# Fused mLSTM, soft-MoE and MLP kernel: the first two chunks' gates, k, q and v loaded apart, decay differences as a bias of the exponentials, gate transpositions in pieces

## The chip, the cores and the metric

One core of one Trainium2 chip. The metric is the device time of one execution in microseconds (us), as a median over runs.

## What is computed

Three stages in a row, in fp32. The first is an mLSTM recurrence over 768 steps for 4 batches of 8 heads with 40 columns each:

```python
m_new = np.maximum(f_gate[:, :, t] + m, i_gate[:, :, t])
f_stab = np.exp(f_gate[:, :, t] + m - m_new)
i_stab = np.exp(i_gate[:, :, t] - m_new)
C = f_stab[..., None, None] * C + i_stab[..., None, None] * np.einsum('bhd,bhe->bhde', vt, kt)
n = f_stab[..., None] * n + i_stab[..., None] * kt
y[:, :, t] = o * np.einsum('bhde,bhe->bhd', C, qt) / np.maximum(np.abs(nq), 1.0)
```

where `nq` is n times q, and `o` the sigmoid of `o_gate`. The 3072 rows of 320 that come out go through a soft mixture of 8 experts with 4 slots each (inner width 1024), and then through an MLP of width 2048 with a squared relu: `g = max(x @ w_in, 0)**2; out = g @ w_out`.

## The kernel before, in words

The recurrence is not stepped. The 768 steps are cut into 6 chunks of 128. The 32 pairs of batch and head go in 11 groups of up to 3 heads. A unit is one group and one chunk. Inside a unit the kernel works with 128 x 128 decay matrices; from chunk to chunk it carries the state. The groups 0 and 1 come first, and their 12 units go by pairs of chunks: chunks 0 and 1 of group 0, of group 1, then chunks 2 and 3 of both, then chunks 4 and 5. Group by group follow the others, then the experts and the MLP.

Before any unit can start, the gates must become decays. `prep(c0, c1)` holds these steps for a stretch of chunks: "1" is chunks 0 and 1, "2" is 2 and 3, "3" is 4 and 5. All operands have 96 rows, three copies of the 32 heads. The letters are:

- f: running sum of the forget gate in each chunk (VectorE scan, L359); i: input gate minus that sum (VectorE, L375); m: running maximum (a copy of the border columns and a scan on VectorE, L364 and L365);
- h, r, u, l, v: the negated maximum in three bf16 parts, stacked in `M3` (L387 on ScalarE, L381 on VectorE, L394 on ScalarE, L375 on VectorE, L396 on ScalarE);
- p: maximum carried in from the chunk before (L370); b and a: differences with the last maximum of the chunk and with the carried one (both are the `sub` helper, L375; b on VectorE, a on GpSimd, as its "G" says); B and A: their exponentials (ScalarE, L378, one instruction for all columns);
- q: TensorE turns the three blocks of 32 rows of each chunk into columns with one 96-wide transposition per chunk (L355), and ScalarE copies both to `qt3` (L356). Column block 0 of `qt3` is the bias of the unit's exponentials, block 1 weighs v, block 2 scales the carried part.

`prep_dec` ("D") makes the carried decay of two chunks in four pieces (L403 and L404, L407, L415 on TensorE, L423).

The units' steps have letters too: M copies a head's row of `M3` over 128 partitions (TensorE, L448); E takes the exponential of it with a bias (ScalarE, L462, three of 128 x 128); K masks the upper triangle (GpSimd, L469); T is k times q (TensorE, L479); P multiplies both (VectorE, L491); W weighs v (GpSimd, L435); U is k times weighted v (TensorE, L510); C is the state's update (VectorE, L526 or L541). `M4` is step M of unit 4, which is group 0 in chunk 2. "~36" is 36 short matmuls on the identity (L203), which compute nothing and only keep TensorE at work.

The order of the start is a string, `START`, written out by hand. Each engine runs its own instructions strictly in the string's order. The part ahead of the first "|" stands before the main loop; each later part is run in one turn of the loop, i = 0, 1, 2 and so on. Turn i issues M of unit i + 3, T of unit i + 2 and U of unit i + 1, then its part of `START`, then P of i + 2 and E of i + 3.

All loads are issued by SyncE (SP), in program order: both gate arrays whole (96 x 768 each, 295 KB), then for groups 0 and 1 three blocks of k, q and the token-wise v and k. The k blocks lie on the diagonal of a block matrix (`kbd`), which must be zeroed first: the first half of group 0 by VectorE (L285), three other quarters by ScalarE (L288, each 120 x 1152). k and q come in two halves of 384 columns.

Of the kernel before, what the change touches and what calls it, by code (L numbers as in the profile page):

```python
# [44 lines left out]
def kernel(  # L45
# [240 lines left out]
    for g, cs in ((1, halves[0]), (0, halves[1]), (1, halves[1])):  # L286
        z = kbd[g][:, :, cs]
        nc.scalar.activation(z, ident[0 : 3 * D, 0:1].unsqueeze(2).to_broadcast(list(z.shape)), AF.Copy, scale=0.0)  # L288
    for g in range(2):
        load_kb(g, halves[0])  # L290
        load_q(g, halves[0])
        load_kv(g)
    for g in range(2):
        load_kb(g, halves[1])
        load_q(g, halves[1])
    nc.sync.dma_start(out=phs, in_=phi)
    load_x(0, range(NC))
# [42 lines left out]
    def prep(c0, c1):  # L340
# [8 lines left out]
        last = mm[32:64, cs, L - 1 : L].to_broadcast([32, w, L])  # L349
# [2 lines left out]
        def qt():
            t = ltb
            for c in range(c0, c1):
                nc.tensor.transpose(t[:, 96 * (c - c0) : 96 * (c - c0) + 96], q3[:, c, :], ident[0:96, 0:96])  # L355
            nc.scalar.copy(qt3[:, cs, :], t[:, 0 : 96 * w].rearrange("p (c s) -> p c s", s=96))  # L356
# [1322 lines left out]
```

## Time and profile before

| | |
|---|---|
| median of 3 runs | 376.58 us (375.27 to 377.73) |
| profiled execution | 376.6 us |
| its span in the trace | 374.9 us |
| TensorE busy | 364.6 us, 97% |
| VectorE, ScalarE, GpSimd busy | 263.5, 258.5, 102.8 us |
| granted TensorE clock | full speed in all 40 slices of the page |

The span runs from the first to the last instruction that the trace shows; 1.7 us of the execution lie around it. A timeline row gives the start in us, the duration in us, the engine, the line, the operation, its output and input with their shapes, and how many instructions were merged; brackets give the idle time ahead of it and what ended that.

### The profile page before, as it was taken

What the parts mean: (1) busy time and instruction counts of PE and PEld (TensorE: products, weight loads), DVE (VectorE), ACT (ScalarE), POOL (GpSimd) and SP (SyncE); (2) the same over time, 40 slices, a digit from 0 to 9 for tenths busy, and PEclk for the clock granted to TensorE, in tenths of its full rate; (3) what the DMA queues carried; (4) which work ended last, traced back from release to release, by engine and by line L of the source; (5) the groups of instructions that cost most, each with busy time, mean ns of one, the idle gap of its engine ahead of it and who ended that gap; (6) DMA issues with size and microseconds to landing.
All of it is one profiled execution on the core that took longest, in us unless ns stands there. A gap on an engine that the chain in (4) does not pass through costs nothing.

```text
span 374.9 us, 10814 instructions
## 1 busy us (share of the span) xinstructions
PE 364.6 (97%) x4203; PEld 325.1 (87%) x4203; DVE 263.5 (70%) x597; ACT 258.5 (69%) x594; POOL 102.8 (27%) x205
## 2 busy tenths in 40 slices
PE   8999999998899999999999999999999999999996
PEld 6789888888779885345999999999999999999995
DVE  8879889986998587886799655555555555555551
ACT  7798776678566865766798756676675666667661
POOL 5576986775687573000000000000000000000000
PEclk9999999999999999999999999999999999999999
DMA  5887998999979999893000200020020001002002
GB/s 183 266 315 217 344 328 238 298 332 347 295 199 397 311 353 365 313 380 130 2 0 2 70 3 0 2 71 2 0 72 1 0 11 60 3 0 73 0 2 70
DMA packets 23004, 56.73 MB, mean 151 GB/s; under 512 B 2865, under 2 KB 9865, under 8 KB 22569
## 3 DMA queue, kind: packets, MB, share of 16 engines
q1 hardware_dynamic: 22953, 56.04, 44.3%
q8 instruction: 33, 0.54, 0.6%
q14 instruction: 18, 0.15, 0.1%
HBM read 52.10 MB, written 3.93 MB: 149 GB/s over the span
## 4 chain that ended last, share of the span: by engine, by line
PE 85%; DVE 5%; ACT 4%; POOL 3%; issue 2%; POOLq 0%
PE ps_mb L1574 19%; PE ps_st L1574 17%; PE ps_lt L1574 9%; PE ps_st L479 8%; PE ps_o L1501 4%; PE ps_o L567 4%; PE ps_o L582 4%; PE ps_st L1389 2%; PE ps_m L1501 2%; ACT w L462 2%; POOL w L469 2%; PE ps_mb L448 2%; PE ps_lt L203 2%; PE ps_st L510 2%; PE ps_lt L733 2%
## 5 line engine op out<-in xcount | busy, mean ns | idle before, releaser
L1525 DVE CAST hi<-ring 128x512 fp32r<-128x512 f32 x93 | 39.7, 427 | 62.0 <-ACT ring L1524 51.8
L1526 DVE TENSOR_TENSOR los<-ring,hi 128x512 fp32r<-128x512 f32 x96 | 66.6, 693 | 9.8
L462 ACT ACTIVATE w<-ps_mb,qt 128x128 f32<-128x128 f32 x192 | 56.4, 368 | 11.5 <-PE ps_mb L448 7.0
L1506 ACT ACTIVATE ring<-ps_o 128x512 f32<-128x512 f32 x64 | 38.2, 597 | 35.0 <-PE ps_o L1501 35.0
L1524 ACT ACTIVATE ring<-ring 128x512 f32<-128x512 f32 x93 | 58.8, 632 | 3.0
L479 PE MATMUL ps_st<-par 120*128 120x128 f32 (+1 forms) x384 | 57.0, 284 | 0.7 <-DVE cu L541 0.6
L1574 PE MATMUL ps_mb<-wohlh,hi 128*128 128x320 f32 x160 | 49.4, 310 | 0.0
L1574 PE MATMUL ps_mb<-wohll,hi 128*128 128x320 f32 x160 | 49.3, 309 | 0.0
L1574 PE MATMUL ps_mb<-wohlh,los 128*128 128x320 f32 x160 | 49.2, 309 | 0.0
L479 PEld LDWEIGHTS ps_st<-par 120*128 120x128 f32 (+1 forms) x384 | 47.9, 191 | 1.2 <-PE ps_mb L448 0.9
L491 DVE TENSOR_TENSOR p<-ps_st,w 128x384 f32<-128x384 f32 (+1 forms) x66 | 35.6, 539 | 16.8 <-POOL w L469 8.2
L469 POOL TENSOR_SCALAR_AFFINE_SELECT w<-w 128x384 f32<-128x384 f32 (+1 forms) x66 | 38.3, 581 | 25.1 <-ACT w L462 23.6
L1574 PE MATMUL ps_st<-wohll,hi 128*128 128x320 f32 x144 | 44.6, 310 | 0.0
L1574 PE MATMUL ps_st<-wohlh,hi 128*128 128x320 f32 x144 | 44.5, 309 | 0.0
L1574 PE MATMUL ps_st<-wohlh,los 128*128 128x320 f32 x144 | 44.5, 309 | 0.0
L1506 ACT ACTIVATE ring<-ps_m 128x512 f32<-128x512 f32 x32 | 19.1, 598 | 19.1 <-PE ps_m L1501 19.1
L1574 PEld LDWEIGHTS ps_mb<-wohll,hi 128*128 128x128 f32 x160 | 29.9, 187 | 1.5
L1574 PEld LDWEIGHTS ps_mb<-wohlh,hi 128*128 128x128 f32 x160 | 30.0, 188 | 0.0
L1574 PEld LDWEIGHTS ps_mb<-wohlh,los 128*128 128x128 f32 x160 | 30.0, 188 | 0.0
L1574 PEld LDWEIGHTS ps_st<-wohll,hi 128*128 128x128 f32 x144 | 27.0, 187 | 2.1 <-issue 0.6
L1574 PEld LDWEIGHTS ps_st<-wohlh,los 128*128 128x128 f32 x144 | 27.1, 188 | 0.0
L1574 PEld LDWEIGHTS ps_st<-wohlh,hi 128*128 128x128 f32 x144 | 27.1, 188 | 0.0
(318 smaller groups left out, 762.2 us busy)
## 6 DMA issues: line engine op xcount, KB each, us to landing
ring<-in_w_dram SPq DMA_DIRECT2D x32, 320.0 KB
stage<-in_w_in_dram SPq DMA_DIRECT2D x10, 512.0 KB
par<-in_w_dram SPq DMA_DIRECT2D x6, 640.0 KB
ring<-in_w_dram SPq DMA_DIRECT2D x6, 640.0 KB
out_dram<-ring SPq DMA_DIRECT2D x24, 160.0 KB
par<-in_k_s_dram SPq DMA_DIRECT2D x9, 360.0 KB
x<-in_o_gate_dram SPq DMA_DIRECT2D x9, 320.0 KB
par<-in_k_t_dram SPq DMA_DIRECT2D x23, 120.0 KB
```

The costliest lines, as they stand in the source:

```text
L462: nc.scalar.activation(w[:, j, :], mb[:, 128 * j : 128 * j + 128], AF.Exp, bias=qt3[:, c, h0 + j : h0 + j + 1])
L469: nc.gpsimd.affine_select(out=w, in_=w, pattern=[[0, nh], [1, 128]], compare_op=ALU.is_ge, fill=0.0, base=0, channel_multiplier=-1)
L479: nc.tensor.matmul(st[:, 128 * j : 128 * j + 128], lhsT=kbd[g % 2][0:nd, j, ts_], rhs=qin[g][0:nd, ts_], start=True, stop=True,)
L491: nc.vector.tensor_tensor(out=p, in0=sts.pop((g, c))[:, 0 : nh * 128].rearrange("p (n t) -> p n t", n=nh), in1=ws.pop((g, c)), op=ALU.mult,)
L567: nc.tensor.matmul(pos[g, c // 2][:, o0 : o0 + nv], lhsT=qin[g][0:nd, 128 * c : 128 * c + 128], rhs=cbds[g, c - 1][0:nd], start=True, stop ...
L582: nc.tensor.matmul(po[t0 : t0 + 32, o0 : o0 + DV], lhsT=p[:, j, t0 : t0 + 32], rhs=vin[g][:, c, j, :], start=True, stop=True,)
L1501: nc.tensor.matmul(t, lhsT=gst[n][:, 128 * k : 128 * k + 128], rhs=cst[tg], start=True, stop=True)
L1506: nc.scalar.activation(r, t, AF.Relu)
L1524: nc.scalar.activation(r, r, AF.Square)
L1525: nc.vector.tensor_copy(hi, r)
L1526: eng.tensor_tensor(out=lo, in0=r, in1=hi.bitcast(F32), op=ALU.subtract)
L1574: nc.tensor.matmul(acc[u][:, 0:DM], lhsT=l_[:, 128 * u : 128 * u + 128], rhs=wohl[r_, f // 8][:, f % 8, :], start=(f == 0 and a == 0), sto ...
```

## The change

- Gates, k, q, v and token-wise k of groups 0 and 1 are loaded for chunks 0 and 1 first (256 columns); the gates of the other four chunks follow behind group 0's first k and q, and the rest of k, q and v (512 columns) behind that (`load_second`).
- The zeroing is cut along the same border and by block: ScalarE writes three blocks of 120 x 256 and three of 120 x 512; GpSimd the last three of 120 x 512. The constant tiles of GpSimd are split the same way, and four copies of the identity (`selF`) move from VectorE to GpSimd.
- Steps a and b go. The exponentials A and B take the difference as bias and scale, one chunk per instruction. A new small step n (VectorE) makes the negated last maximum.
- Besides q there are s, t and w: transpositions of row block 0 alone, of block 1 (rows 0 to 63 with the copy of 32 to 63), and of all 96 rows with the copy of block 2. s is copied by ScalarE, t and w by VectorE.
- `START` is written anew, with 32 filling matmuls in place of 55. Two small VectorE pieces (`heads`) move into it.

```diff
-START = "~36 1f 1i 1m 1h 1p 1b 1aG 1B 1r 1u 1A 1v D0 2f 1l T0 T1 1q M0 2i E0 W0 K0 D0 M1 E1 ~6 2m D0 2p 2b 2aG K1 W2 P0 2h D0 2B 2r 2u U0 P1 M2 2v E2 2A 2l K2 C0 ~7 | 3f 3i D1 ~6 | D1 2q 3m 3h 3p | D1 3b 3aG 3B 3r | 3u D1 3A 3l 3v | D2 3q | D2 | D2 | D2 X |"
+START = "~13 1f 1i 1s ~9 1m 1h 1p 1n 1r 1u 1v H D0 1l T0 M0 T1 1B 2f M1 E0 H 2i 1t K0 W0 D0 E1 ~9 2m 1A 2h P0 2r D0 2u K1 W2 U0 D0 P1 2l 2v 2p 2n M2 E2 K2 C0 L ~1 | 1w 2s 2B 3f | 2t D1 3i D1 | D1 3m 2A | D1 3h 3p 3n 2w 3r 3u | 3l 3v 3A D2 | 3s 3B 3t D2 | D2 3w | D2 X |"
...
-    nc.sync.dma_start(out=fg.rearrange("p c s -> p (c s)"), in_=f_gate)
-    nc.sync.dma_start(out=ig.rearrange("p c s -> p (c s)"), in_=i_gate)
-    halves = slice(0, S // 2), slice(S // 2, S)
+    def load_gates(c0, c1):
+        for t, src in ((fg, f_gate), (ig, i_gate)):
+            nc.sync.dma_start(
+                out=t[:, c0:c1].rearrange("p c s -> p (c s)"), in_=src[:, L * c0 : L * c1]
+            )
...
+    load_gates(0, 2)
+    halves = slice(0, 2 * L), slice(2 * L, S)
...
+    for g in (1, 0):
+        for j in range(3):
+            zero(g, j, halves[1 - g])
+    zeros = []
+    for j in range(3):
+        zeros.append(lambda j=j: nc.gpsimd.memset(kbd[1][:, j, halves[1]], 0.0))
+    load_kb(0, halves[0])
+    load_q(0, halves[0])
+    load_gates(2, NC)
+    load_kv(0, 0, 2)
+    load_kb(1, halves[0])
+    load_q(1, halves[0])
+    load_kv(1, 0, 2)
...
+        if r < 3:
+            nc.vector.tensor_copy(sel96[rs, :], ident[rs, rs])
+        nc.gpsimd.tensor_copy(selF[rs, :], ident[rs, rs])
...
+        def qt(r=0, n=96):
+            t = bank("o") if n == 64 and c0 == 0 else ltb
             for c in range(c0, c1):
...
+                nc.tensor.transpose(t[:, n * (c - c0) : n * (c - c0) + n], q3[0:n, c, :], ident[0:n, 0:n])
+            tv = t[:, 0 : n * w].rearrange("p (c s) -> p c s", s=n)
+            (nc.vector.tensor_copy if r else nc.scalar.copy)(qt3[:, cs, r:n], tv[:, :, r:])
...
-            return lambda: nc.scalar.activation(q3[r : r + 32, cs], q3[r : r + 32, cs], AF.Exp)
+            def go():
+                for c in range(c0, c1):
+                    src, b, k = (q3, mlast, 1.0) if r == 32 else (mm, mprev, -1.0)
+                    nc.scalar.activation(
+                        q3[r : r + 32, c], src[r : r + 32, c], AF.Exp, bias=b[r : r + 32, c], scale=k
+                    )
...
-            "a": sub(q3[64:96, cs], mprev[64:96, cs].to_broadcast([32, w, L]), mm[64:96, cs]),
-            "b": sub(q3[32:64, cs], q3[32:64, cs], last),
+            "n": last,
...
+            "s": qt32,
+            "t": lambda: qt(32, 64),
+            "w": lambda: qt(64),
```

On ScalarE, between the zeroing (`par`) and the first units' exponentials (`w`), there stands before (`M_112` is `M3`, `ring` holds the gates, `qt_113` is `qt3`):

```order
L387 ACTIVATE M_112<-ring 96x256
L378 ACTIVATE ring<-ring 32x256
L394 CAST M_112<-ring 32x256
L378 ACTIVATE ring<-ring 32x256
L396 CAST M_112<-ring 32x256
L404 ACTIVATE ring<-ring 32x2
L356 COPY qt_113<-ps_lt 128x192
L462 ACTIVATE w<-ps_mb,qt_113 128x128 x6
```

and with the change:

```order
L291 ACTIVATE par_71<-ident 120x256 x3
L291 ACTIVATE par_70<-ident 120x512 x3
L392 COPY qt_113<-ps_m 128x2x32
L435 ACTIVATE M_112<-ring 96x256
L441 CAST M_112<-ring 32x256
L443 CAST M_112<-ring 32x256
L454 ACTIVATE ring<-ring 32x2
L422 ACTIVATE ring<-ring 32x128 x2
L512 ACTIVATE w<-ps_mb,qt_113 128x128 x6
L422 ACTIVATE ring<-ring 32x128 x2
```

The copy of the transposed block moved ahead of h, the two decay exponentials moved behind u and v; one of them (A, the last row) stands behind the six exponentials of units 0 and 1.

On VectorE, from the step r of chunks 0 and 1 to the step l of chunks 2 and 3, whose output `M4` reads, there stands before:

```order
L403 TENSOR_TENSOR ring<-ring 32x2
L359 SCALAR_TENSOR_TENSOR ring<-ring 96x256
L375 TENSOR_TENSOR M_112<-ring,M_112 32x256
L375 TENSOR_TENSOR ring<-ring 96x256
L407 TENSOR_TENSOR ring<-ring 32x22
L364 COPY ring<-ring 96x2
L365 SCALAR_TENSOR_TENSOR ring<-ring 96x256
L370 TENSOR_TENSOR ring<-ring 96x2
L375 TENSOR_TENSOR ring<-ring 32x256
L491 TENSOR_TENSOR p<-ps_st,w 128x384
```

and with the change:

```order
L411 TENSOR_TENSOR M_112<-ring,M_112 32x256
L395 SCALAR_TENSOR_TENSOR ring<-ring 96x256
L360 COPY ring<-ring 32x120
L411 TENSOR_TENSOR ring<-ring 96x256
L386 COPY qt_113<-ps_o 128x2x32
L457 TENSOR_TENSOR ring<-ring 32x22
L400 COPY ring<-ring 96x2
L401 SCALAR_TENSOR_TENSOR ring<-ring 96x256
L541 TENSOR_TENSOR p<-ps_st,w 128x384
L429 SCALAR_TENSOR_TENSOR ring<-ring,M_112 96x256
```

The step l of chunks 0 and 1 moved ahead of the next stretch's scan, two steps (p, b) ahead of the first product P went, and two copies came in. Behind the product both orders go on with r, the copy of the carried decay, the second product and step l.

On GpSimd, at the end of its constants and up to the first mask K, there stands before:

```order
L322 MEMSET selJ 32x128
L323 COPY selJ<-ident 32x4x8
L375 TENSOR_TENSOR ring<-ring 32x256
L435 TENSOR_TENSOR wv<-par_70,qt_113 128x246
L469 AFFINE_SELECT w<-w 128x384
```

and with the change (of its zeroing only the last row):

```order
L301 MEMSET par_71 120x512 x3
L338 MEMSET hm 120x3
L339 AFFINE_SELECT hm<-hm 120x3
L342 AFFINE_SELECT hm<-hm 120x3
L345 MEMSET rmask 128x4
L347 MEMSET rmask 32x1 x4
L348 MEMSET selJ 32x128
L349 COPY selJ<-ident 32x4x8
L354 COPY selF<-ident 32x32 x4
L519 AFFINE_SELECT w<-w 128x384
```

Step a went, the zeroing and the four copies came in, and the first K stands ahead of the first W.

## Rows read from the trace of the kernel before

**Rows 1.** The page, its first line.
```profile
span 374.9 us, 10814 instructions
```
**Rows 2.** Windows: busy us of each engine, granted clock, DMA share, GB/s.
```profile
14.38:22.60 8.22, 7.72 (x152) 6.84 (x151) 7.79 (x23) 6.02 (x21) 5.29 (x9) 1.00 0.86 306
22.60:35.00 12.40, 12.40 (x281) 11.57 (x281) 9.85 (x26) 12.25 (x36) 8.71 (x17) 1.00 0.79 247
90.50:95.00 4.50, 3.15 (x64) 2.84 (x53) 1.77 (x6) 2.90 (x9) 2.59 (x7) 1.00 0.99 358
```
**Rows 3.** The chain of waits up to 30 us: start, us, what.
```profile
7.94 1.34 PE ps_st L479 x12
9.28 0.18 PE ps_lt L355 x2
...
10.79 0.71 POOL w L469
...
13.51 0.82 DVE M L375
```
**Rows 4.** Timeline, 0 to 20 us: the gates' path and units 0 to 6.
```profile
1.42 6.51 PE L203 MATMUL ps_lt<-ident 128*128 128x256 bf16 x36 [1.42 <-POOL dm L280]
...
2.20 3.25 ACT L288 ACTIVATE par<-ident 120x1152 f32<-120x1152 f32 x3
...
4.04 0.69 DVE L359 TENSOR_TENSOR_SCAN ring<-ring 96x256 f32<-96x256 f32 x1
...
4.97 0.42 DVE L375 TENSOR_TENSOR ring<-ring 96x256 f32<-96x256 f32 x1 [0.25 <-DMA ring<-in_i_gate_dram]
...
5.01 0.46 POOL L323 COPY selJ<-ident 32x32 f32<-32x32 f32 x1
...
5.56 0.69 DVE L365 TENSOR_TENSOR_SCAN ring<-ring 96x256 f32<-96x256 f32 x1
...
6.29 0.42 ACT L387 ACTIVATE M<-ring 96x256 bf16<-96x256 f32 x1 [0.84 <-DVE ring L365]
...
6.99 0.73 DVE L381 SCALAR_TENSOR_TENSOR ring<-ring,M 96x256 f32<-96x256 f32 x1
...
8.41 0.42 DVE L375 TENSOR_TENSOR M<-ring,M 32x256 bf16<-32x256 f32 x1
...
9.21 0.17 DVE L407 TENSOR_TENSOR ring<-ring 32x22 f32<-32x22 f32 x1
...
9.28 0.50 PE L448 MATMUL ps_mb<-M,sel 96*128 96x128 bf16 x6
...
9.83 1.66 ACT L462 ACTIVATE w<-ps_mb,qt 128x128 f32<-128x128 f32 x6
...
11.53 0.56 DVE L491 TENSOR_TENSOR p<-ps_st,w 128x384 f32<-128x384 f32 x1 [0.44 <-POOL w L469]
...
14.39 0.34 PE L448 MATMUL ps_mb<-M,sel 96*128 96x128 bf16 x3
...
18.84 0.33 PE L448 MATMUL ps_mb<-M,sel 96*128 96x128 bf16 x3 [0.31 <-ACT w L462]
```
**Rows 5.** Windows of TensorE in the first us, with DMA share and GB/s.
```profile
1.40:2.00 0.60, 0.58 (x3) 1.00 0.44 61
2.00:3.00 1.00, 1.00 (x7) 1.00 0.79 277
...
4.00:5.00 1.00, 1.00 (x6) 1.00 0.14 42
```
**Rows 6.** Waits of the DMA queue (SP), 0 to 60 us: total, times, longest.
```profile
SPq L213 <- ACT par L288: 1.9, 1, 1.9
```
**Rows 7.** Groups by shape: count, busy us, mean ns of one, idle before.
```profile
L305 POOL MEMSET ring<- 96x768 f32 x1 | 0.7, 727 | 0.0
...
L1506 ACT ACTIVATE ring<-ps_o 128x512 f32<-128x512 f32 x64 | 38.2, 597 | 35.0 <-PE ps_o L1501 35.0
```
**Rows 8.** Timeline at 92 us: a matmul in the middle of a group.
```profile
91.98 0.22 PE L582 MATMUL ps_o<-par,p 128*32 128x41 f32 x1 [1.35 <-issue]
```

More of the change, by code (lines that the diff above doesn't have):

```diff
@@ L281, with zero, load_second @@
     nc.scalar.activation(dm, dm, AF.Exp)
-    nc.sync.dma_start(out=fg.rearrange("p c s -> p (c s)"), in_=f_gate)
-    nc.sync.dma_start(out=ig.rearrange("p c s -> p (c s)"), in_=i_gate)
-    halves = slice(0, S // 2), slice(S // 2, S)
-    nc.vector.memset(kbd[0][:, :, halves[0]], 0.0)
[L286 to L297, printed above, removed]
+    def load_gates(c0, c1):
[3 more added lines that the diff above has]
+            )
+    def zero(g, j, cs):
+        z = kbd[g][:, j, cs]
+        nc.scalar.activation(z, ident[0 : 3 * D, 0:1].to_broadcast(list(z.shape)), AF.Copy, scale=0.0)
+    load_gates(0, 2)
+    halves = slice(0, 2 * L), slice(2 * L, S)
+    nc.vector.memset(kbd[0][:, :, halves[0]], 0.0)
+    for g in (1, 0):
[11 more added lines that the diff above has]
+    load_kv(1, 0, 2)
+    def load_second():
+        for g in range(2):
+            load_kb(g, halves[1])
+            load_q(g, halves[1])
+            load_kv(g, 2, NC)
+        nc.sync.dma_start(out=phs, in_=phi)
+        load_x(0, range(NC))
     nc.gpsimd.memset(gj, 1.0)
@@ L304 @@
     rst = gt(96, [NC, L])
-    nc.gpsimd.memset(rst, 1.0)
-    nc.gpsimd.memset(rst[:, :, 0:1], 0.0)
     dl = gt(96, [NC, L])
-    nc.gpsimd.memset(dl, 0.0)
-    nc.gpsimd.memset(dl[:, 0, 0:1], NEG)
     mprev = gt(96, [NC, 1])
-    nc.gpsimd.memset(mprev, NEG)
+    mlast = gt(96, [NC, 1])
+    for c0, c1 in ((0, 2), (2, NC)):
+        nc.gpsimd.memset(rst[:, c0:c1], 1.0)
+        nc.gpsimd.memset(rst[:, c0:c1, 0:1], 0.0)
+        nc.gpsimd.memset(dl[:, c0:c1], 0.0)
+        if c0 == 0:
+            nc.gpsimd.memset(dl[:, 0, 0:1], NEG)
+            nc.gpsimd.memset(mprev, NEG)
+        else:
+            for z in zeros:
+                z()
     nc.gpsimd.memset(hm, 1.0)
@@ L348, in prep, with qt32 @@
         tail = mm[:, c0 - 1, L - 1 : L] if c0 else 0.0
[L349 removed]
         tt = {"D": nc.vector.tensor_tensor, "G": nc.gpsimd.tensor_tensor}
[L352 to L353 removed]
+        def qt(r=0, n=96):
+            t = bank("o") if n == 64 and c0 == 0 else ltb
             for c in range(c0, c1):
[L355 to L356 removed]
+                nc.tensor.transpose(t[:, n * (c - c0) : n * (c - c0) + n], q3[0:n, c, :], ident[0:n, 0:n])
+            tv = t[:, 0 : n * w].rearrange("p (c s) -> p c s", s=n)
+            (nc.vector.tensor_copy if r else nc.scalar.copy)(qt3[:, cs, r:n], tv[:, :, r:])
+        def qt32():
+            t = bank("m")
+            for c in range(c0, c1):
+                nc.tensor.transpose(t[:, 32 * (c - c0) : 32 * (c - c0) + 32], q3[0:32, c, :], ident[0:32, 0:32])
+            nc.scalar.copy(qt3[:, cs, 0:32], t[:, 0 : 32 * w].rearrange("p (c s) -> p c s", s=32))
         def f_scan():
@@ L375, in sub, with last @@
             return lambda e="D": tt[e](out=o_, in0=a, in1=b, op=ALU.subtract)
+        def last():
+            nc.vector.tensor_scalar(
+                out=mlast[32:64, cs], in0=mm[32:64, cs, L - 1 : L], scalar1=-1.0, scalar2=None, op0=ALU.mult
+            )
         def exp(r):
-            return lambda: nc.scalar.activation(q3[r : r + 32, cs], q3[r : r + 32, cs], AF.Exp)
+            def go():
+                for c in range(c0, c1):
+                    src, b, k = (q3, mlast, 1.0) if r == 32 else (mm, mprev, -1.0)
+                    nc.scalar.activation(
+                        q3[r : r + 32, c], src[r : r + 32, c], AF.Exp, bias=b[r : r + 32, c], scale=k
+                    )
+            return go
         def rest():
@@ L922 @@
     begin["W"] = lambda n: e_wv(units[int(n)][0], 0, 2)
+    hd = heads()
+    begin["H"] = lambda: next(hd, None)
+    begin["L"] = load_second
     begin["X"] = lambda: nc.vector.tensor_copy(sel4, selF.unsqueeze(1).to_broadcast([128, 4, 32]))
```

10 lines of the change are left out of this document (5 added, 5 removed).

## The prediction

> **What bounds the kernel now.** I read the page first: the span is 374.9 us [rows 1], and the execution that it comes from took 376.6 us, which is the median of the runs (376.58) to within 0.02. So 1.7 us lie around the span, and a sum made on the span can be set against the median as it is. Then I cut the span into stretches. From 14.38 us on TensorE is the bound: it is busy 7.72 of 8.22 us up to 22.60 and 12.40 of 12.40 up to 35 [rows 2]. All code that the change touches runs ahead of or in these stretches. So the question is how much earlier TensorE can start the first instruction of that unbroken run, which is `M4` at 14.39 [rows 4], and what the change adds to TensorE's own work behind it.
>
> The chain of waits says what `M4` waited for: VectorE's step l of chunks 2 and 3, 13.51 to 14.33 [rows 3]. Going back from there in the timeline one finds the gates' path: the input gate lands and step i starts at 4.97, m at 5.56, h at 6.29, r at 6.99, l at 8.41, `M0` at 9.28, the first exponentials E at 9.83 [rows 4], the first mask K at 10.79 [rows 3], the first product P at 11.53 [rows 4].
>
> **The gates' load.** The two gate arrays are 590 KB. The windows show 61 GB/s x 0.6 us = 37 KB up to 2.0 us, then 277 KB in the next us; the queue falls to 42 GB/s between 4 and 5 us [rows 5], so the last of them was moved near 4.3, and step i, which waited for it, started 0.65 us later [rows 4]. With the change 197 KB come first. At the same rate they are through at 2.0 + (197 - 37) / 277 = 2.6 us and land near 3.3; the forget gate, the first half of them, near 3.1. The scan f (0.69) then ends at 3.8, and i starts there in place of 4.97: 1.15 us earlier. The trace shows no small load by itself, so the bounds are wide: nothing gained if a fixed time sets the landing, 1.6 if both land as the bytes do. I take 1.15. m then ends at 5.1.
>
> **ScalarE's zeroing.** Three instructions of 1152 columns fill 2.20 to 5.45 [rows 4]. In their place come three of 256 columns at 0.42 (as h, [rows 4]) and three of 512 at 0.60 [rows 7]: 3.06 us, to 5.26. Ahead of h now stands the copy of step s, some 0.25 (64 columns against h's 256). So h starts at 5.5, not at 5.1: 0.8 earlier than 6.29. Of the 1.15 us a third is lost here, and ScalarE becomes what is late.
>
> **From h to the first product.** Steps a and b no longer stand between. h 0.42, r 0.73, u and then l 0.42 each, four gaps of some 0.03: l ends at 7.55 and `M0` starts at 7.6, 1.7 earlier than 9.28. On ScalarE v (0.42) ends at 7.5, then come one small exponential (0.2) and two of B. One instruction of 128 columns with a bias is seen in E: 1.66 for six, 0.28 each [rows 4]; the one over 256 columns that a pair replaces I take at 0.42, as h. So a pair is 0.56, 0.14 more, and E starts at 8.4 in place of 9.83.
>
> GpSimd must have its constants ready by then. Before, they end at 5.47, behind the copy of 5.01 [rows 4]. The change adds three memsets of 512 columns (0.73 x 512 / 768 = 0.49 each [rows 7]), four copies (at most 0.46 each, as that one [rows 4]) and a few small memsets, some 0.3: 5.5 + 1.5 + 1.8 + 0.3 = 9.1. E's first three end at 8.4 + 0.83 = 9.25. So GpSimd is just in time, and K starts at 9.3 in place of 10.79.
>
> The Trainium skill says in "GPSIMD Engine Reference", section Key points, that GpSimd shares its SBUF interfaces with VectorE and contends with VectorE instructions that have two SBUF inputs. By that rule the four copies would come later still than the sum of their durations, since r and l, which have two inputs, run beside them.
>
> VectorE has from l's end seven instructions ahead of the first P: two scans (0.69 each), one subtraction (0.42) and four small ones (0.17 as the one at 9.21 [rows 4], call it 0.2): 2.6, with gaps 2.85. P starts at 7.55 + 2.85 = 10.4, 1.1 earlier than 11.53. Here VectorE is late, no longer the mask. Behind it come P 0.56, r 0.73, a small copy 0.2, the second P 0.56 and l 0.42, with gaps 2.6: l of chunks 2 and 3 ends at 13.0, against 14.33. TensorE is there in time. From `M0` to `M4` it now needs 14.39 - 9.28 = 5.1 us; nine filling matmuls fewer stand there (0.18 each, 6.51 us for 36 [rows 4]), and one T more (1.34 / 2 = 0.67) and three pairs of transpositions (0.18 [rows 3]): 5.1 - 1.6 + 0.7 + 0.5 = 4.7, so it is there at 7.6 + 4.7 = 12.3. So `M4` starts at 13.0, **1.4 us earlier**.
>
> **Behind it, on TensorE.** ScalarE is then 1.4 ahead as well, so the 0.31 that TensorE waits at 18.84 [rows 4] goes. On the other side, in the turns from i = 1 on, the pieces t, w, s, t, w take the place of two whole transpositions: three pairs more. A pair of the 96-wide kind is 0.18 in the chain [rows 3]; the narrower ones are not in the trace, between 0.1 and 0.33; I take 0.18, so 0.55 in all. Net 1.4 + 0.3 - 0.55 = 1.15 us.
>
> **ScalarE behind it.** Between 22.60 and 35 it is busy 12.25 of 12.40 us [rows 2]. Step B of chunks 4 and 5 moves into this stretch whole, 0.56. If ScalarE sets the pace there, this comes off, and 0.55 is left of 1.15; if TensorE does, nothing. I take the middle: **0.9 us**, 375.7 us.
>
> **The loads behind.** SP waits 1.9 us for ScalarE's zeroing of a neighbouring block [rows 6], and that is the hole between 4 and 5 us. With the zeroing cut along the loads SP needs no such wait for group 0. The bytes are the same, five issues more. What the units from `T4` on read then comes up to 1.5 us earlier than now; I cost it at nothing, since TensorE shows no wait for a load in the stretches of rows 2. If this cover were gone (1 KB rows moving slower than 3 KB ones) the first to be late would be `T4`.
>
> **The rivals.**
>
> *Absorbed.* The queue is full near 90 us (0.99 of the engines' time, 358 GB/s, TensorE busy only 3.15 of 4.50 us [rows 2]). If the loads set the pace there, TensorE comes earlier and waits longer, and nothing is left: 376.6. For it: the share of 0.99. Against: the wait inside the group of L582 is not put down to a load ("issue" [rows 8]), and the loads start earlier too. The same time comes out if ScalarE binds at 22 to 35 us and the small ops are each 0.05 longer.
>
> *More.* The loads that start earlier also remove the stall of 1.35 us ahead of the matmul at 91.98 [rows 8]. Then 0.9 + 1.35 = 2.25: 374.3. For it: the stall lies where the queue is full. Against: nothing in the trace ties it to a load.
>
> *TensorE's clock falls, slower.* 23 of the 55 filling matmuls go. In the trace of before the granted clock is full (1.00, the 2.4 GHz level) in each stretch of rows 2 and 5, and TensorE has hardly a gap from 1.42 us on. With the change it waits more: some 0.8 us ahead of `M0` and about 1.5 us in all up to `M4`. Should the clock fall to the lower level (1.2 GHz) there, a unit of 2.2 us (18.84 minus 14.39, over two [rows 4]) becomes up to 4.4. From 0.4 of a unit on (0.9 / 2.2) the gain is eaten; with two units the time is 376.6 - 0.9 + 4.4 = 380.1. Against it: the gaps are short beside the work, and nothing in the trace shows the lower level.
>
> The Trainium skill, "TensorE: Matmul & The Clock Gate", section "HAM oscillation — how this bites in real kernels", says that waits between bursts of matmuls can put the array back to half rate; no stretch of this trace shows that, so the rule speaks for this rival and no row does.
>
> **How the numbers follow.** Forecast (0.55 to 1.4 us gained) 0.52; absorbed 0.27; more 0.13; clock 0.08. A measurement of this kernel tells about 1%, 3.8 us, from no change. No case reaches 372.8, save more stalls than the one falling away: 0.03. The clock case passes 380.3 from a little over two units on, about half of it: 0.04. The rest is within 1%: 0.93. The range runs from 374.0, a little below the case "more", to 377.8, which takes in the absorbed case with the spread of three runs (1.1 us above the median) and nearly one unit at the lower clock (376.6 - 0.9 + 2.2 = 377.9).
>
> **What would show it.** Right: step i near 3.8, h near 5.5 directly behind ScalarE's copy, `M0` near 7.6, E near 8.4, the first P near 10.4 with VectorE busy ahead of it, `M4` near 13.0, the granted clock at 1.00 throughout, and the work at 60 us some 0.9 earlier. Wrong: step i still near 4.9 (a fixed landing time); the first K waiting for GpSimd's copies rather than for E; `M4` earlier by 1.4 but the work at 60 us not; a stretch at the lower clock; `T4` waiting for a load.

## The result, and the profile after

The changed kernel takes 380.52 us (median of 6 runs, 379.42 to 384.21), the kernel before in the same comparison 376.38 (6 runs, 374.69 to 377.73). The ratio is 1.0116, 95% interval 1.008 to 1.0151: 4.1 us slower, where 0.9 less was forecast. The profiled execution took 379.54 us, with a span of 377.8 (against 374.9, [rows 1]), so 1.7 us lie around it as before. TensorE's busy time and granted clock in 40 slices, from the page:

```profile
span 377.8 us, 10830 instructions
...
PE   7979999999899999999999999999999999999996
...
PEclk9989999999999999999999999999999999999999
```

The third clock digit stands for 18.9 to 28.3 us; it was a 9 before, as all 40 were, and is the first sign of where the time went. But the front did what was forecast. The timeline of the changed kernel (start, duration, engine; L411 is `sub`, so steps i and l; L401 m, L435 h, L429 r, L498 M, L512 E, L519 K, L541 P), to be held against [rows 4]:

```profile
3.93 0.42 DVE L411 TENSOR_TENSOR ring<-ring 96x256 f32<-96x256 f32 x1
4.52 0.69 DVE L401 TENSOR_TENSOR_SCAN ring<-ring 96x256 f32<-96x256 f32 x1
5.24 0.42 ACT L435 ACTIVATE M<-ring 96x256 bf16<-96x256 f32 x1 [0.17 <-DVE ring L401]
5.69 0.42 DVE L429 SCALAR_TENSOR_TENSOR ring<-ring,M 96x256 f32<-96x256 f32 x1
7.12 0.34 PE L498 MATMUL ps_mb<-M,sel 96*128 96x128 bf16 x3 [0.54 <-DVE M L411]
8.01 1.66 ACT L512 ACTIVATE w<-ps_mb,qt 128x128 f32<-128x128 f32 x6
9.03 0.54 POOL L519 TENSOR_SCALAR_AFFINE_SELECT w<-w 128x384 f32<-128x384 f32 x1 [0.43 <-ACT w L512]
10.03 0.52 DVE L541 TENSOR_TENSOR p<-ps_st,w 128x384 f32<-128x384 f32 x1
13.13 0.33 PE L498 MATMUL ps_mb<-M,sel 96*128 96x128 bf16 x3 [0.32 <-DVE qt L386]
17.60 0.53 DVE L541 TENSOR_TENSOR p<-ps_st,w 128x384 f32<-128x384 f32 x1
```

Step i starts 1.04 us earlier than before, the first P 1.50, `M4` 1.26, and the product of unit 4 (last row) 2.11, since before it started at 19.71. Then the lead goes. I count it with the start of each unit's product P on VectorE, "P8" for unit 8: P6 is 1.16 earlier than before, P7 1.38 later, P8 3.51 later, P12 2.95 later, and so it stays up to 90 us. Five us are lost between P4 and P12.

The first hold is on ScalarE in turn 3 (L441 is u, L443 v, L422 the exponentials A and B, L653 a copy of a unit's result, L751 a sigmoid of the gate o):

```profile
17.71 0.42 ACT L435 ACTIVATE M<-ring 96x256 bf16<-96x256 f32 x1
20.17 0.40 ACT L441 CAST M<-ring 32x256 bf16<-32x256 f32 x1 [2.05 <-DVE ring L429]
20.59 0.88 ACT L512 ACTIVATE w<-ps_mb,qt 128x128 f32<-128x128 f32 x3
...
24.47 0.69 ACT L422 ACTIVATE ring<-ring 32x128 f32<-32x128 f32 x2
```

In turn 3 `START` now has h, p, n, w, r and u of chunks 4 and 5 in one heap. u waits for r, and behind u stand the exponentials of unit 6, which were ready. VectorE does not come to r before 19.71, because between h's end (18.13) and r it has its own units' steps and three of the heap (L406 p, L414 n, L386 the copy of w):

```profile
18.58 0.29 DVE L406 TENSOR_TENSOR ring<-ring 96x2 f32<-96x2 f32 x1
18.88 0.55 DVE L414 TENSOR_SCALAR ring<-ring 32x2 f32<-32x2 f32 x1
19.46 0.22 DVE L386 COPY qt<-ps_lt 128x64 f32<-128x64 f32 x1
19.71 0.42 DVE L429 SCALAR_TENSOR_TENSOR ring<-ring,M 96x256 f32<-96x256 f32 x1
```

The second hold is in TensorE's queue in turn 5. The transposition t (L384) reads B, and B stands on ScalarE behind unit 7's exponentials, the copy L653, the sigmoid and the copy of s. Behind t stand AV (L632, decay times v), the carried part (L617), M and T (L529):

```profile
21.20 0.46 PE L617 MATMUL ps_o<-ring,par 120*128 120x123 f32 x2 [0.61 <-DVE ring L669]
...
24.93 0.66 PE L384 MATMUL ps_lt<-ident,ring 64*128 64x64 f32 x2 [1.47 <-ACT ring L422]
25.52 1.05 PE L632 MATMUL ps_o<-par,p 128*32 128x41 f32 x48
26.49 0.79 PE L617 MATMUL ps_o<-ring,par 120*128 120x123 f32 x2
27.07 0.53 PE L498 MATMUL ps_mb<-M,sel 96*128 96x128 bf16 x3
27.39 1.50 PE L529 MATMUL ps_st<-par 120*128 120x128 f32 x6
```

The last column shows the waits of 0.61 and 1.47; the durations show the third loss. T took 0.89 in turns 1 to 4 and takes 1.50 here. The windows of this stretch (length, then busy us and count of PE, PEld, DVE, ACT and POOL, granted clock, DMA share, GB/s) say why, against the 12.40 of 12.40 at 1.00 in [rows 2]:

```profile
20.00:22.00 2.00, 1.09 (x9) 0.84 (x8) 1.62 (x6) 1.75 (x6) 0.39 (x1) 1.00 1.00 375
22.00:24.00 2.00, 1.46 (x13) 1.23 (x12) 1.06 (x3) 1.99 (x8) 0.78 (x3) 1.00 1.03 405
24.00:26.00 2.00, 1.05 (x31) 0.80 (x34) 0.42 (x4) 1.95 (x8) 0.66 (x3) 0.81 0.51 176
26.00:28.00 2.00, 2.00 (x43) 1.85 (x33) 0.83 (x3) 1.61 (x5) 1.15 (x3) 0.50 0.02 6
28.00:30.00 2.00, 2.00 (x17) 1.84 (x16) 0.24 (x2) 1.69 (x5) 0.52 (x1) 0.84 0.74 246
```

TensorE was busy 1.09, 1.46 and 1.05 of 2 us, and then its clock was at the lower of its two levels (0.50, 1.2 GHz) for some 3.4 us (2 x 0.19 / 0.5 in the third window, all of the fourth, 2 x 0.16 / 0.5 in the fifth). The five groups from t to T are 1.82 us longer than the same groups at full clock (0.32 + 0.38 + 0.31 + 0.20 + 0.61).

### The profile page after: what moved, and what is told of

It is laid out like the page before. It is cut to its first block, busy times and chain, and to the rows that moved or that the text cites. A ratio compares the mean times of both kernels' runs of the same rounds, so it can differ in the third digit from the quotient of the medians.

```text
span 377.8 us, 10830 instructions
## 1 busy us (share of the span) xinstructions
PE 364.9 (97%) x4192; PEld 324.6 (86%) x4192; DVE 263.1 (70%) x601; ACT 259.6 (69%) x603; POOL 103.0 (27%) x212
## 3 DMA queue, kind: packets, MB, share of 16 engines
HBM read 52.10 MB, written 3.93 MB: 148 GB/s over the span
## 4 chain that ended last, share of the span: by engine, by line
PE 79%; DVE 8%; ACT 5%; DMA 2%; issue 2%; POOL 2%; SPq 1%; POOLq 0%; DVEq 0%; ACTq 0%
PE ps_mb L1627 19%; PE ps_st L1627 17%; PE ps_lt L1627 9%; PE ps_st L529 8%; PE ps_o L1554 4%; PE ps_o L632 4%; PE ps_o L617 3%; DVE p L541 2%; PE ps_mb L498 2%; PE ps_st L1442 2%; PE ps_st L560 2%; PE ps_m L1554 2%; DMA x<-in_w_out_dram 2%; ACT w L512 1%; DVE x L714 1%
## 5 line engine op out<-in xcount | busy, mean ns | idle before, releaser
L512 ACT ACTIVATE w<-ps_mb,qt 128x128 f32<-128x128 f32 x192 | 56.5, 369 | 12.6 <-PE ps_mb L498 7.4
L529 PE MATMUL ps_st<-par 120*128 120x128 f32 (+1 forms) x384 | 57.8, 286 | 0.9 <-DMA par<-in_k_t_dram 0.7
L529 PEld LDWEIGHTS ps_st<-par 120*128 120x128 f32 (+1 forms) x384 | 48.6, 194 | 1.3 <-PE ps_mb L498 1.3
L519 POOL TENSOR_SCALAR_AFFINE_SELECT w<-w 128x384 f32<-128x384 f32 (+1 forms) x66 | 38.2, 579 | 28.6 <-ACT w L512 23.4
L541 DVE TENSOR_TENSOR p<-ps_st,w 128x384 f32<-128x384 f32 (+1 forms) x66 | 35.5, 538 | 14.2 <-POOL w L519 6.6
```

The costliest lines, as they stand in the source:

```text
L512: nc.scalar.activation(w[:, j, :], mb[:, 128 * j : 128 * j + 128], AF.Exp, bias=qt3[:, c, h0 + j : h0 + j + 1])
L519: nc.gpsimd.affine_select(out=w, in_=w, pattern=[[0, nh], [1, 128]], compare_op=ALU.is_ge, fill=0.0, base=0, channel_multiplier=-1)
L529: nc.tensor.matmul(st[:, 128 * j : 128 * j + 128], lhsT=kbd[g % 2][0:nd, j, ts_], rhs=qin[g][0:nd, ts_], start=True, stop=True,)
L541: nc.vector.tensor_tensor(out=p, in0=sts.pop((g, c))[:, 0 : nh * 128].rearrange("p (n t) -> p n t", n=nh), in1=ws.pop((g, c)), op=ALU.mult,)
```

## The experiments

My theory after the two traces: the front's gain is real, and it is lost because most steps of chunks 4 and 5 come one to three turns later than before and stand in heaps. In before, m and h are in turn 1, r and B in turn 2, u at the head of turn 3; in the changed kernel m is in turn 2, h, r and u in turn 3 (u at its end), B in turn 5. Rivals: the three additional transpositions and the split exponentials cost this wherever they stand; fewer filling matmuls let the clock fall; the new loads bring something in late.

All results, with the kernel before at 376.2 to 376.8 us in the same comparisons. M4 and P are starts in us from the profiled execution; "clock" is the lowest granted clock in a window of 2 us between 18 and 30 us.

| kernel | median us | ratio (95%) | M4 | P4 | P8 | P12 | clock |
|---|---|---|---|---|---|---|---|
| before | 376.4 | 1 | 14.39 | 19.71 | 26.40 | 33.36 | 1.00 |
| changed | 380.52 | 1.0116 (1.008 to 1.0151) | 13.13 | 17.60 | 29.91 | 36.31 | 0.50 |
| e1_u_late | 377.95 | 1.0026 (0.9992 to 1.006) | 13.14 | 17.60 | 29.20 | 35.61 | 0.50 |
| e2_B_early | 377.04 | 0.9991 (0.9971 to 1.0012) | 13.74 | 18.20 | 27.27 | 33.68 | 1.00 |
| e3_both | 376.60 | 0.9981 (0.996 to 1.0002) | 13.14 | 17.60 | 26.39 | 32.79 | 1.00 |
| e4_fill | 378.35 | 1.0034 (1.0009 to 1.0059) | 13.15 | 17.61 | 28.43 | 34.84 | 1.00 |
| e5_front_early_prep3 | 377.04 | 1.0013 (0.9982 to 1.0044) | 13.13 | 17.89 | 26.09 | 33.52 | 1.00 |
| e6_old_order | 375.84 | 0.9976 (0.9949 to 1.0004) | 13.07 | 17.93 | 24.96 | 31.92 | 1.00 |
| e6_again | 375.64 | 0.9981 (0.996 to 1.0001) | 13.66 | 18.53 | 25.55 | 32.51 | 1.00 |
| e7_old_order_late3 | 379.81 | 1.0084 (1.0053 to 1.0115) | 13.06 | 17.13 | 27.82 | 36.93 | 0.50 |
| e8_loads_only | 378.02 | 1.0045 (1.0018 to 1.0072) | 15.65 | 20.33 | 27.09 | 34.05 | 1.00 |
| e9_bias_only | 376.71 | 1.0016 (0.9997 to 1.0035) | 14.18 | 18.89 | 25.77 | 32.73 | 1.00 |
| e10_B_late | 375.38 | 0.9976 (0.9953 to 0.9999) | 13.90 | 18.72 | 25.60 | 32.56 | 1.00 |
| e11_fewer_fill | 374.98 | 0.996 (0.9938 to 0.9982) | 13.27 | 18.10 | 24.98 | 31.93 | 1.00 |

**Single holds taken out of the changed kernel.** First u behind the exponentials of unit 6:

```diff
-| D1 3h 3p 3n 2w 3r 3u | 3l 3v 3A D2 |
+| D1 3h 3p 3n 2w 3r | 3u 3l 3v 3A D2 |
```

> One edit to the changed kernel: step u of chunks 4 and 5 moves from the end of turn 3 to the head of turn 4, as it stood before. Theory 'order' (ScalarE, held 2.05 us by u at 18.1 us, starts the exponentials of units 6 to 8 late, so step B of chunks 4 and 5 is late and TensorE waits 1.5 us in its queue for the transposition t): the hold on ScalarE falls below 0.5 us, TensorE's wait ahead of t below 0.8 us, the clock stays at 1.00, and the time falls from 380.5 to about 375.7 us. Rival 'clock' (with fewer filling matmuls TensorE's clock falls on its own, whatever the order): the lower clock stays somewhere between 20 and 30 us, time 378 to 380.5. Rival 'bias' (the split exponentials load ScalarE too much): the hold goes, but exponentials start no earlier, 379 or more.

Then B early, ahead of r:

```diff
-| D1 3h 3p 3n 2w 3r 3u | 3l 3v 3A D2 | 3s 3B 3t D2 |
+| D1 3h 3p 3n 2w 3B 3r 3u | 3l 3v 3A D2 | 3s 3t D2 |
```

> One edit to the changed kernel: step B of chunks 4 and 5 moves from turn 5 to turn 3, ahead of step r; u stays where it holds ScalarE. Theory 'order': the hold of some 2 us on ScalarE stays (B now is part of it), but TensorE no longer waits for B ahead of t (below 0.3 us in place of 1.5) and the 0.96 us by which unit 7 is ahead stays: about 375.5 us, clock at 1.00 or lower for a short time. Rival 'clock': the lower clock still shows and the time stays above 378. Rival 'bias': no gain, 380.

Then both:

```diff
-| D1 3h 3p 3n 2w 3r 3u | 3l 3v 3A D2 | 3s 3B 3t D2 |
+| D1 3h 3p 3n 2w 3r | 3u 3B 3l 3v 3A D2 | 3s 3t D2 |
```

> Two edits to the changed kernel: step u of chunks 4 and 5 to the head of turn 4 and step B from turn 5 to directly behind it. Theory 'order': neither the hold on ScalarE nor TensorE's wait ahead of t is left, the 1.26 us by which M4 starts earlier reach the end: about 375.0 us, below both kernels, clock at 1.00. Rival 'clock': 378 or more. Rival 'absorbed' (the queue is full near 90 us): the work at 60 us is 1.2 us earlier than in the kernel before, but the end is not, 376.4.

And the holds left alone, with TensorE kept at work over them by 12 more filling matmuls:

```diff
-| 3l 3v 3A D2 | 3s 3B 3t D2 |
+| ~3 3l 3v 3A D2 | 3s 3B ~9 3t D2 |
```

> The changed kernel with filling matmuls where TensorE stands still: 3 at the head of turn 4, 9 ahead of the transposition t in turn 5; the waits themselves stay. Theory 'order': the waits of ScalarE and TensorE stay as they are (the hold of 2.0, t at 24.9 us), but the clock stays at 1.00, so the first matmuls behind t lose their extra 1.3 us or somewhat more: 378.0 to 379.0 us and less spread between runs. Rival 'clock' as the main cause: all 4 us come back, 376 or less. If the fillers themselves are late (9 at 0.13 to 0.18), 380.5.

(e2 is 0.6 later than the others already at `M4`; that is no part of its edit, see the last section.) With u late the hold of 2.05 is 1.08 and no longer stands ahead of unit 6's exponentials (18.22 for 20.59), but TensorE still waits for B, 0.97 us, and its clock falls behind that. This profiled execution is not the usual one: of e1's ten, eight kept a mean clock of 0.998 or more (377.4 to 378.7 us), and two, this one among them, had 0.989 and 0.986 (379.4 and 381.9 us). With B early the wait for B is gone and the clock stays at 1.00, though TensorE still stands 0.60 and 0.32 us at 21 and 22 us. With both, P8 is at before's time. So each hold is a cause, and in the profiled executions the clock fell behind the one in TensorE's queue. All three came out slower than forecast (375.7, 375.5 and 375.0 us), and none can be told from the kernel before: without the holds the loss is gone, but the front's gain is not there either. e4 prices the clock alone. Its TensorE comes to t at the same time as in the changed kernel, and then goes on at full clock:

```profile
23.40 1.16 PE L203 MATMUL ps_lt<-ident 128*128 128x256 bf16 x9
24.95 0.56 PE L384 MATMUL ps_lt<-ident,ring 64*128 64x64 f32 x2 [0.40 <-ACT ring L422]
25.44 0.67 PE L632 MATMUL ps_o<-par,p 128*32 128x41 f32 x48
```

It is 2.2 us faster than the changed kernel (380.52 to 378.35; 2.6 when each is held against the kernel before of its own comparison) and still 0.1 to 0.6% slower than before. So of the 4.1 us some 2.2 to 2.6 are the clock, and the rest, 1.6 to 2.0, the waits and what they push back.

**The steps of chunks 4 and 5 early, with the new front.** e5 takes everything of `START` behind the first "|" apart:

```diff
-| D1 3m 2A | D1 3h 3p 3n 2w 3r 3u | 3l 3v 3A D2 | 3s 3B 3t D2 | D2 3w | D2 X |
+| D1 3m 3n 3h | D1 3r 3B | 3u 3s 3l 3v 3p D2 | 3t D2 2A | 2w D2 | D2 X | 3A | 3w |
```

> After's front word for word; behind it the steps of chunks 4 and 5 go back to the turns in which the kernel before had them (m, n, h in turn 2, r and B in turn 3, u, s, l, v in turn 4), and the steps that only the carried part of later units needs (p, t, w, A of chunks 4 and 5, w of chunks 2 and 3, A of chunks 2 and 3) go back to turns 4 to 10. Nothing is left out. Theory deferral (the front's gain is real, and after loses it because the steps of chunks 4 and 5 come one turn later and in one heap, behind which ScalarE and TensorE's queue stand): no hold of over 1 us on ScalarE in turn 3 and none of over 1 us on TensorE ahead of t; the ninth product P (P8) about 1.0 us earlier than before's 26.40 where after has it 3.51 later; granted clock 1.00 from 18 to 30 us; 375.6 us. Theory pieces (the three more pairs of transpositions and the split exponentials cost what the front gains, wherever they stand): P8 within 0.5 of before's, 376.6 to 377. Theory clock alone (fewer filling matmuls in the front let the clock fall, whatever stands in the turns): a stretch at 0.5 between 20 and 30 us again, 379 or more.

A miss in size. The long holds and the fall of the clock are gone, but P8 is 0.31 earlier than before and not 1.0, and the time is before's. Its trace has u at 20.67, behind B (19.06) and unit 6's exponentials (19.77), and TensorE waiting 0.51 for v ahead of `M8` at 21.79. What this kernel lacks against the next one (the three pieces, or the places of these steps) was not separated.

**The old order.** e6 has the changed loads and zeroing and the bias of the exponentials, but before's order with one whole transposition q:

```diff
+START = "~30 1f 1i 1m 1h 1p 1n 1B 1r 1u 1A 1v H D0 2f 1l T0 T1 1q M0 2i E0 H W0 K0 D0 M1 E1 ~6 2m D0 2p 2n K1 W2 P0 2h D0 2B 2r 2u U0 P1 M2 2v E2 2A 2l K2 C0 L ~7 | 3f 3i D1 ~6 | D1 2q 3m 3h 3p | D1 3n 3B 3r | 3u D1 3A 3l 3v | D2 3q | D2 | D2 | D2 X |"
```

> After's loads and zeroing, and the differences as bias of the exponentials (a and b dropped), but the order of before: the whole transposition q in place of s, t and w, 30 filling matmuls ahead (36 before). Nothing is left out. Theory deferral: the order of before has no step put off, so nothing is to be given back: M4 0.9 to 1.1 us earlier than before's 14.39 and the products from P8 on earlier by about the same; granted clock 1.00; 375.6 us. Theory pieces: nothing speaks against this one either. Rival (TensorE or ScalarE is the bound from M4 on whatever the front does, so that an earlier front is absorbed between P4 and P8): M4 1.0 earlier, P8 and what follows within 0.3 of before, 376.5.

> The kernel of e6_old_order once more, unchanged, to narrow its interval: 0.9976 [0.9949, 1.0004] there, and 374.9 us in its profiled execution. If the 1.43 us by which its products are earlier reach the end, the ratio is 1 - 1.43 / 376.5 = 0.996, between 0.994 and 0.998.

e8 is e6 without the bias, with before's a, b and exponentials; in its string

```diff
-1p 1n 1B
+1p 1b 1aG 1B
```

and so for chunks 2 to 5. e9 is the kernel before with the opposite edit, the bias alone.

> The kernel of e6_old_order with the old steps a and b (b on VectorE, a on GpSimd) and one exponential for all columns in place of one per chunk: of the change only the loads and the zeroing in pieces are left, in the order of before. Nothing is left out. If the loads make the gain of the front, M4 comes 0.7 to 1.0 us earlier than before's 14.39, and e6 is within 0.3 us of it. If the bias makes it (no subtraction of 0.42 on VectorE ahead of the first product, no wait of B for it), M4 is here only 0.3 to 0.5 earlier, and e6 0.5 us faster. Time by the first 375.8 us, by the second 376.2.

> The kernel before with the differences as bias of the exponentials alone (step n in place of b and a, one exponential per chunk); loads, zeroing, order as before. Nothing is left out. If loads and bias each add their share: e8_loads_only had P8 0.69 later than before and e6_old_order 1.44 earlier, so the bias alone would give 2.1 us: P8 near 24.3, 374.5 us. If the bias was worth so much there only because the loads apart had made GpSimd late for step a (8.53 there, 6.60 in before): M0 about 0.3 earlier than 9.28, M4 0.3 to 0.5 earlier than 14.39, P8 near 26.0, 376.1 us.

e6 is what the front's gain is worth where nothing is put off: `M4` at 13.07, as early as with the new order (13.13), P8 and P12 1.44 earlier than before and every product up to 90 us by the same. In this execution the rival that an earlier front is absorbed from `M4` on falls. The same steps as above stand in e6 without a hold:

```profile
18.72 0.27 ACT L653 COPY ring<-ps_o 128x123 f32<-128x123 f32 x1
19.01 0.40 ACT L441 CAST M<-ring 32x256 bf16<-32x256 f32 x1
19.32 0.68 ACT L422 ACTIVATE ring<-ring 32x128 f32<-32x128 f32 x2
20.03 0.40 ACT L443 CAST M<-ring 32x256 bf16<-32x256 f32 x1
```

e8 was a miss: I expected the loads to make the gain, and alone they make the kernel slower. Its first product comes at 12.53, 1.00 later than before. The rows of GpSimd and ScalarE say why (L411 on GpSimd is step a, L419 its exponential):

```profile
7.17 1.27 POOL L354 COPY selF<-ident 32x32 f32<-32x32 f32 x4
...
8.53 0.61 POOL L411 TENSOR_TENSOR ring<-ring 32x256 f32<-32x256 f32 x1
```

```profile
9.17 0.41 ACT L419 ACTIVATE ring<-ring 32x256 f32<-32x256 f32 x1 [2.32 <-POOL ring L411]
```

The zeroing and the four copies that the new loads bring to GpSimd push step a from 6.60 to 8.53. The bias removes step a. So the loads need the bias: alone (with their zeroing) they cost 1.6 us by the medians, 0.2 to 0.7% by the interval. The bias alone (e9) cannot be told from no change; its products are 0.63 earlier in the profiled execution. VectorE no longer has step b ahead of r, which starts 0.25 earlier, and r takes 0.42 us where before it took 0.73, beside step a on GpSimd; the two were not separated. Together they gave -0.6 and -0.5 us in two comparisons, both just short of being told from nothing.

**The suspected cause added to e6.** The decisive run: the steps of chunks 4 and 5 put off to the turns of the changed kernel, and nothing else.

```diff
-| 3f 3i D1 ~6 | D1 2q 3m 3h 3p | D1 3n 3B 3r | 3u D1 3A 3l 3v | D2 3q |
+| 3f D1 ~6 | D1 2q 3i | D1 3m | 3h 3p 3n 3r 3u D1 | 3l 3v 3A D2 | 3B 3q D2 |
```

> The kernel of e6_old_order with one edit: the steps of chunks 4 and 5 are put off to the turns in which the changed kernel has them (i in turn 1, m in turn 2, h to u in turn 3, l, v, A in turn 4, B and q in turn 5). Nothing is left out. Theory deferral: the hold on ScalarE in turn 3 (u behind h, over 1 us) and the one in TensorE's queue in turn 5 (ahead of q) come back; products from P8 on 2.5 to 4.5 us later than in e6_old_order (that is 1 to 3 later than before's), with a stretch at the lower clock if the gaps are as long as the changed kernel's; 377.5 to 379.5 us. Theory pieces or front (the loss comes from the three more transpositions, the fewer filling matmuls or the new front): none of these is in this kernel, so the products stay within 0.5 us of e6_old_order's, 375.8 us.

379.81 us, 4.2 above e6 in the same comparison (375.64) and close to the changed kernel, though it has e6's front, fillers and whole transpositions. Both holds are back, at the places named, with 1.79 and 1.47 us. ScalarE:

```profile
19.44 0.40 ACT L441 CAST M<-ring 32x256 bf16<-32x256 f32 x1 [1.79 <-DVE ring L429]
```

TensorE, with T at 1.59 behind it:

```profile
24.09 0.59 PE L384 MATMUL ps_lt<-ident,ring 96*128 96x96 f32 x2 [1.47 <-ACT ring L422]
...
25.71 1.59 PE L529 MATMUL ps_st<-par 120*128 120x128 f32 x6
```

and the windows:

```profile
22.00:24.00 2.00, 0.62 (x6) 0.43 (x4) 1.21 (x4) 1.99 (x8) 0.88 (x2) 1.00 0.91 326
24.00:26.00 2.00, 1.91 (x56) 1.60 (x57) 0.54 (x3) 1.57 (x7) 0.39 (x1) 0.92 0.34 103
26.00:28.00 2.00, 2.00 (x10) 1.78 (x9) 0.18 (x1) 2.00 (x6) 0.88 (x2) 0.50 0.66 177
```

Its twelve runs also price the two parts apart: three kept a mean clock of 1.00 and took 377.0 to 377.2 us, nine had 0.985 to 0.994 and took 378.6 to 382.4. So the putting off costs some 1.4 us against e6 (375.64) by itself, and the executions in which the clock falls take 1.5 to 5.3 more. Not all of that is due to the holds: the profiled one also has a wait of 0.81 us inside AV at 18.7 us, put down to nothing ("issue"), and a second fall of the clock at 97 to 101 us (see the last section). The changed kernel's six runs all have a mean clock of 0.987 to 0.995.

**A version that beats both.** e10 is e6 with B of chunks 2 and 3 behind unit 2's exponentials:

```diff
-D0 2B 2r 2u U0 P1 M2 2v E2 2A 2l
+D0 2r 2u U0 P1 M2 2v E2 2l 2B 2A
```

> The kernel of e6_old_order with B of chunks 2 and 3 behind the exponentials of unit 2 in place of ahead of them. Nothing is left out. M4 waits in e6_old_order until ScalarE has read unit 2's bank (12.14 to 13.02), and ScalarE gets there 0.7 late because of B. Theory: M4 0.5 to 0.7 earlier than 13.07, and the products from P8 on 0.3 to 0.6 earlier than there, 375.4 us. Rival: B and A together (1.4 us) then stand ahead of unit 3's exponentials and of the transposition q, and the products from P8 on come out within 0.2 of e6_old_order or later, 375.8 us or more.

e11 is e10 with 22 fillers ahead:

```diff
-START = "~30 1f
+START = "~22 1f
```

> The kernel of e10_B_late with 22 filling matmuls ahead in place of 30. Nothing is left out. Theory: in the executions seen the first filling matmuls take 0.21 us each and later ones 0.11, and the moment at which they become short differs from one execution to the next; 30 of them ended at 6.72 in e6_old_order and at 7.63 in e10_B_late, and everything behind them (T of units 0 and 1, the transposition, M0 at 8.06 against 8.97) came later by as much. With 22 they end by 6.2 in any case, M0 is set by the decay exponentials at 7.8 to 8.1, and the products from P8 on are 1.4 to 1.8 us earlier than before's 26.40 in every execution: 375.0 us, ratio 0.996. Rival: TensorE gets idle ahead of the transposition and its clock is late or falls for it, a stretch under 1.00 or the matmuls of units 0 to 3 at their long durations: 376 us or more.

e10's profiled execution was a miss for `M4`, at 13.90. It was 0.9 late from its first T on, ahead of the edit, and the reason is TensorE's pace in the first us. The same 30 fillers in e6 and in e10:

```profile
1.43 5.29 PE L203 MATMUL ps_lt<-ident 128*128 128x256 bf16 x30 [1.43 <-POOL dm L280]
```

```profile
1.43 6.20 PE L203 MATMUL ps_lt<-ident 128*128 128x256 bf16 x30 [1.43 <-POOL dm L280]
```

What B's place is worth was therefore not settled (375.38 against 375.84 and 375.64). In e11 the fillers are through before they can be in the way:

```profile
1.43 4.51 PE L203 MATMUL ps_lt<-ident 128*128 128x256 bf16 x22 [1.43 <-POOL dm L280]
...
7.89 0.49 PE L498 MATMUL ps_mb<-M,sel 96*128 96x128 bf16 x6
```

e11 takes 374.98 us, ratio 0.996 (0.9938 to 0.9982): 1.4 us faster than before and 5.5 faster than the changed kernel. Its products are 1.42 us earlier than before's at P8 and 1.43 at P12, as much as the time is shorter.

## Why the prediction was wrong

- **The gates' load**: right. i at 3.93 for the forecast 3.8.
- **ScalarE's zeroing, from h to the first product**: right in the main, most of it a little better. h 5.24 for 5.5 (the six pieces took 2.56 us, not 3.06), `M0` 7.12 for 7.6, E 8.01 for 8.4, the first P 10.03 for 10.4, `M4` 13.13 for 13.0. GpSimd's copies ended at 8.60, and the first K waited for E, as forecast. A pair of exponentials was 0.69 us, not 0.56, and the terms from h to l add up to an end at 7.61, not 7.55; neither mattered.
- **"Behind it, on TensorE"**: this is the step that failed. It priced the steps of chunks 4 and 5 by what their instructions last (0.55 us for three pairs of transpositions; they took 0.26 each, 0.78, as later pairs do in before's own trace, 15.75 to 16.01; the 0.18 of [rows 3] was only a pair's share of the chain) and took the new places for free. It did not ask, for each moved step, which instruction waits there and what stands behind it. The products went from 2.11 us early at P4 to 3.51 late at P8, and e7 shows that the new places alone cost 4.2 us (1.4 where the clock held).
- **"ScalarE behind it"**: of the same kind. I saw that ScalarE is busy 12.25 of 12.40 us and that B moves into this stretch, and weighed B's 0.56 us. What counted was that t waits for B in TensorE's own queue, and that u waits for r ahead of unit 6's exponentials. Both rows of the order, h and u in one turn and B and t in one turn, could be read from `START` before.
- **The rival "absorbed"**: it fell. In e6 the whole 1.44 us goes through to 90 us; in e6_again 0.85 go through to 46 us, are lost there in a stall that the profile does not explain (P21 is 0.03 later than before), and are back at the last product (0.97 earlier). Single executions differ by so much behind 45 us, and e6's medians are only 0.6 and 0.5 us shorter. The firmer evidence is e11, where 1.42 us at P8 came out as 1.4 us (0.7 to 2.3 by the interval).
- **The rival "more"**: not borne out. Behind 90 us the lead grew (from 1.42 to 2.01 us in e6, from 1.40 to 1.80 in e11), but in e9 too, which has the loads of before (from 0.62 to 1.31). So nothing ties this to the earlier loads.
- **The rival "TensorE's clock falls"**: the mechanism came, and 380.1 was near the time, but for another place and partly by chance. I looked for gaps ahead of `M0` and up to `M4`; there the granted clock was 1.00. It fell at 24 to 29 us, after gaps that my step above did not see. Its own price was some 2.2 to 2.6 us (e4), not 4.4, and the rest were waits. The Trainium skill, "TensorE: Matmul & The Clock Gate", section "HAM oscillation — how this bites in real kernels", which the prediction weighed, says that waits between bursts of matmuls can put the array back to half rate; these traces agree (0.50 at 26 to 28 us, in the changed kernel, e1 and e7), though the waits ahead of the fall, 0.61, 0.30 and 1.47 us in the changed kernel, were shorter than those of the page's case.
- **"The work at 60 us some 0.9 earlier"**: the product that starts at 60.97 us in before came 2.95 later; without the putting off (e6) 1.43 earlier.

## What to carry to other kernels

When a hand-written order is changed, write down for every instruction that moves on an in-order queue what it waits for in its new place and which ready instruction stands behind it; a step that lasts 0.4 us held an engine for 2 us here. Put off only what nobody waits for, and keep the producer of an operand (B) a turn ahead of the instruction that heads another queue (t). An engine whose clock can fall pays a second time for such a wait, so read the clock of the windows behind a change of order too. And test parts alone as well as together: the loads, which were the point of this change, alone made the kernel slower until the bias took a step off GpSimd.
